# Attention and a gated MLP on one core: the second of four sequences in chunks of 384 tokens in place of 256, with the gating products' second slot and the value means in other places

## The chip, the cores and the metric

The kernel runs on one core of a Trainium2 chip. The metric is the device time of one execution in microseconds (us). The engines are named as the profile names them: PE multiplies matrices (PEld is its loading of weights), DVE, ACT and POOL work element by element, and SP issues DMAs here, one after the other and in the order of its program; a DMA whose buffer or data is not ready holds up every DMA behind it on SP. Each engine has such an order of its own.

## The reference

Two steps. First an attention over 4 sequences, 8 heads, 768 positions and 64 values a head, in which each query sees the keys within 15 positions of it and, for the whole sequence, 24 summaries, one for each block of 32 positions: the maximum of the keys in the block and the mean of the values.

```python
k_sum = k.reshape(B, H, nb, block, D).max(axis=3)
v_sum = v.reshape(B, H, nb, block, D).mean(axis=3)
scores_l = scale * np.matmul(q, k.transpose(0, 1, 3, 2))
mask_l = np.abs(pos[:, None] - pos[None, :]) < window      # window = 16
scores_s = scale * np.einsum('bhsd,bhnd->bhsn', q, k_sum) + np.log(block)
scores_all = np.concatenate([np.where(mask_l, scores_l, -1e9), scores_s], axis=-1)
a = softmax(scores_all)
out = np.matmul(a, np.concatenate([v, v_sum], axis=2))
```

Then a gated MLP over the 3072 rows of 512 that come out: `(x @ w_a) * (x @ w_b) @ w_out`, with 1536 hidden values. All is in fp32.

## The kernel before

**The MLP.** The 3072 tokens are 24 tiles of 128, six for each sequence, and the tiles are grouped in chunks of two (256 tokens, "narrow") or three (384, "wide"). `chunks` lists them: the first two sequences have three narrow chunks each, the last two have two wide ones each, ten in all. For a chunk `u` the MLP runs over 12 blocks `f` of 128 hidden values; one pair (u, f) is an item. All weights stay in SBUF. To reach fp32 precision each operand is split in a high and a low part, and a product is made of three: an item has 24 up products on PE (L1046, `h<-x,w`, 12 for each of w_a and w_b; `late` is the same input at another place), then the gating on ACT and DVE (copy, multiply, and the split of the result into `gh` and `gl`), and later the down products (L1123, `o<-w,gh`, `gl` and `x`), 3 for each of its tiles. In narrow items the gating products have two slots, taken in turn; the second slot, `last`, lies in a ninth place of the input buffer `xt`, so the profile calls it x. Wide items use one slot, of full width. When a chunk's twelfth item is done, its tiles are copied from PSUM to SBUF (L1169, L1175) and stored (`out_dram<-S`, one DMA for each tile).

**The attention of a chunk** is done while the MLP of earlier chunks runs. For each tile: load the queries (`qin<-in_q`), transpose them on DVE (L998, `qT<-qin`), scores on PE (L637, `c<-kT,qT`), softmax on DVE, ACT and POOL, transposes of the weights on DVE (L774, `pt<-s`), values on PE (L790, `o<-pt,vw`), and the split of the result into the chunk's inputs `x`. The buffer qin holds two tiles. A narrow chunk loads its queries for both tiles at once, in 16 DMAs of 32x8x32 elements (32 KB), a wide one tile by tile, in 16 DMAs of 32x4x32 (16 KB). The values of a tile and the summaries stand together in vw, which has one buffer: its three loads for a tile (`vw<-in_v`) follow the value product of the tile before. At the beginning of a sequence its keys are loaded, transposed and reduced (`prep_keys`), and its value means are made (`prep_values`): loads of v into S (`S<-in_v`), sums on POOL into vm, eight small DMAs, one for each head, from vm to a place in S (`S<-vm`, `summed(b)`), and from there two DMAs into vw (`vw<-S`).

**The order.** The kernel is written out by a small planner, `Work`. Every operation has a rank, an assumed duration, and the names of what it reads and writes; the planner gives each engine, when it is free, the ready operation of lowest rank, and so fixes the order of each engine's program. The first operations of each engine follow a list of numbers, `ORDER`, which the change leaves as it is. The planner takes 0.45 us for the issue of any load on SP. Ranks of SP's loads: 90 for S<-in_v and out_dram, 97 for vw, 98 for queries, 99 for S<-vm. An operation "-" takes no engine; it stands for a wait on all that it names.

Of the kernel before, what the change touches and what calls it, by code (L numbers as in the profile page):

```python
# [136 lines left out]
def attention_moe(  # L137
# [11 lines left out]
    B, H, S, D = q.shape  # L149
    P = 128  # L150
# [6 lines left out]
    NS = S // BLK  # L157
# [3 lines left out]
    G = CH // P  # L161
    WIDE = 3

    chunks = [(b, t, n) for b, n in enumerate((G, G, WIDE, WIDE)) for t in range(0, S // P, n)]
    NU = len(chunks)
    CV = 512
    AHEAD = (15, 19, 35)
# [4 lines left out]
    FILL = 2  # L172
# [64 lines left out]
        nc.vector.memset(vbuf[e], 0.0)  # L237
    nc.vector.memset(sbuf[:, :, :, COLS:], 0.0)
    xt = sb([P, 9, NP, P], "x", F32R)
    last = xt[:, 8].rearrange("p c x -> p (c x)")  # L240
    gt, ght, glt = sb([P, 2 * CH], "g"), sb([P, WIDE * P], "gh", F32R), sb([P, WIDE * P], "gl", F32R)
    gs = [gt[:, i * CH : (i + 1) * CH] for i in range(2)]
    ghs, gls = [ght[:, :CH], last[:, :CH]], [glt[:, :CH], last[:, CH:]]
# [20 lines left out]
    def homes_of(u):  # L264
        n = chunks[u][2]
        if u <= FILL:
            return [[f"X{u % 2 * 2 * G + p * G + i}" for i in range(n)] for p in range(2)]
        if u % 2:
            return [[f"X{6 + i}" for i in range(n)], [f"S0.{i}" for i in range(n)]]
        return [[f"X{p * WIDE + i}" for i in range(n)] for p in range(2)]  # L270
# [8 lines left out]
        return late[0][:, : len(names)]  # L279

    def summed(b):
        x = spaces["S0"][:NS, 2 * CV : 3 * CV] if b == 1 else spaces["S1"][4 * NS : 5 * NS, 3 * CV :]
        return x.rearrange("p (h d) -> p h d", d=D)

    def slot(space, i):
        return spaces[space][:, i * 512 : (i + 1) * 512], f"{space}.{i}"
# [32 lines left out]
    def load(rank, kb, rate, reads, writes, out, in_):  # L319
        work.add(  # L320
            "SP", rank, 0.45, kb, reads, writes,
            lambda: nc.sync.dma_start(out=out, in_=in_), rate=rate,  # L322
        )
# [183 lines left out]
    def prep_keys(b):  # L507
        rank = LATER + 2 * b - 0.5
        if b == 1:
            work.add("-", 0, 0, 0, (), ["S1.2", "S1.3", "S0.2", *PU], lambda: None)  # L510
        for c in range(NP):
            i = c % 2 if b == 1 else 0
            kw = kins[i]
            more = (["lo25"], ["S1.2", "S1.3"])[i]
            keys = blocks(96, f"kin{i}", kw, k, b, c, -16, more) + more * i
            groups = kw[:, :S].rearrange("p (i x) -> p i x", x=P)
            for takes, o, i in (
                (0.7, kper[:, c, :, :WIN], groups[:, :, :WIN]),
                (0.26, kper[:, c, :, COLS:], groups[:, :, WIN:]),
                (0.15, kT[:, c, KC - 32 :], kw[:, S:]),  # L520
            ):
                dve(
                    rank, takes, keys, [f"kT{c}k"] + (KB if b == 1 else []),
                    lambda o=o, i=i: nc.vector.transpose(out=o, in_=i),
                )

            hv = half.rearrange("p i x -> p (i x)")
            x16 = "p i (n x) -> p i n x"
            for takes, o, i in (
                (0.65, half[:, :, :6], kper[:, c, :, :WIN].rearrange(x16, x=16)),  # L530
                (0.26, half[:, :, 6:], kper[:, c, :, COLS:].rearrange(x16, x=16)),
                (0.1, ks[:, c, NS - 1, None], kT[:, c, KC - 32 : KC - 16]),
            ):
                dve(
                    rank, takes, [f"kT{c}k"], [f"ks{c}", "half"],
                    lambda o=o, i=i: nc.vector.tensor_reduce(out=o, in_=i, axis=AX.X, op=ALU.max),
                )
            last = ks[:, c, NS - 1, None]
            for takes, o, i0, i1 in (
                (0.26, ks[:, c, : NS - 1], hv[:, 1 : 2 * NS - 2 : 2], hv[:, 2 : 2 * NS : 2]),  # L540
                (0.1, last, last, hv[:, 2 * NS - 1, None]),
            ):
                dve(
                    rank, takes, (), [f"ks{c}", "half"],
                    lambda o=o, i0=i0, i1=i1: nc.vector.tensor_tensor(
                        out=o, in0=i0, in1=i1, op=ALU.max
                    ),
                )
            summaries(rank, c)

    def prep_values(b):


        T = 8

        at, keys, rank = (0, ["S1.0", "S1.1"], LATER) if b == 1 else (3, ["S1.3"], 50)
        x = spaces["S1"][: 4 * NS, at * CV :]

        def add(n, out, i0, i1, writes):
            pool(  # L560
                rank, 0.15 + n / 450, (), writes,
                lambda: nc.gpsimd.tensor_tensor(out=out, in0=i0, in1=i1, op=ALU.add),  # L562
            )

        room = ["S0.2"] if b == 1 else []
        for hg in range(2):
            vv = v[b, 4 * hg : 4 * hg + 4].rearrange("h (n t) d -> (h n) t d", t=BLK)
            y, pk = vm[: 4 * NS, hg], f"vm{hg}"
            for i in range(BLK // T):
                j = i % len(keys)  # L570
                load(
                    90, 197.0, 150, (), [keys[j]],
                    x[:, j * T * D : (j + 1) * T * D].rearrange("p (t d) -> p t d", d=D),
                    vv[:, i * T : (i + 1) * T, :],
                )
                if j == len(keys) - 1:
                    n = len(keys) * T * D // 2
                    while n > D:
                        add(n, x[:, :n], x[:, :n], x[:, n : 2 * n], keys)
                        n //= 2  # L580
                    if i == j:
                        add(n, y, x[:, :n], x[:, n : 2 * n], keys + [pk])
                    else:
                        add(n, x[:, :n], x[:, :n], x[:, n : 2 * n], keys)
                        add(n, y, y, x[:, :n], keys + [pk])
            pool(
                rank, 0.37, (), [pk],
                lambda y=y: nc.gpsimd.tensor_scalar(
                    out=y, in0=y, scalar1=1.0 / BLK, scalar2=None, op0=ALU.mult
                ),  # L590
            )
            for h in range(4):
                load(
                    99, 6.0, 20, [pk] + room, [VS[4 * hg + h]],
                    summed(b)[:, 4 * hg + h], y[h * NS : (h + 1) * NS],
                )
# [182 lines left out]
    def products(u, t, vw, vk, bk, pt=None):  # L779

        rank = rank_of(u)
        ps = bank[bk].rearrange("p (c x) -> p c x", x=P)
        d, dk = pt or PD

        def fn():
            for c in range(NP):
                for e in range(2):
                    es = slice(e * QT, (e + 1) * QT)
                    for h in range(2):
                        nc.tensor.matmul(  # L790
                            ps[h * D : (h + 1) * D, c, es], vw[e][:COLS, 2 * c + h, :],
                            d[:COLS, h, c, es], start=True, stop=True, tile_position=(0, h * D),
                        )

        def split():
            i = t - chunks[u][1]
            hk, lk = (names[i] for names in homes_of(u))
            also = []
            if u == FILL + 1:
                also = PU + [f"S0.{j}" for j in range(4) if j != i] if i == 0 else []  # L800

            y = ps.rearrange("p c (b a) -> p c a b", a=2)

            def home(part):
                return inputs_of(u, part)[:, i].rearrange("p c (a b) -> p c a b", a=2)

            act(
                CHAIN if u > FILL else rank, 0.52, [bk], [hk] + ["gh1", "gl1"] * (hk == "X8"),
                lambda: nc.scalar.copy(out=home(0), in_=y),
            )  # L810
            dve(
                CHAIN if u > FILL else rank, 0.6, [bk, hk], [lk] + (also if i == 0 else []),
                lambda: nc.vector.tensor_tensor(
                    out=home(1), in0=y, in1=home(0).bitcast(F32), op=ALU.subtract
                ),
            )

        return dk[0] + dk[1] + vk, bk, fn, split
# [144 lines left out]
    def attention(u):  # L963
# [18 lines left out]
        def bring(i):  # L982
            load_values(b, t0 + i, vbuf, VK[:3], 97)
            if t0 == 0 and i == 0:
                for e, r0 in ((0, WIN), (1, 32)):
                    load(97, 49.0, 100, VS + (["S0.2"] if b == 1 else []), [VK[3 + e]], vbuf[e][r0 : r0 + NS], summed(b))

        def begin(i):
            keys = list(qk)
# [72 lines left out]
    def item(n, u, f):  # L1062
# [27 lines left out]
        else:  # L1090
# [4 lines left out]
            gk, bk, end = ["g0", "g1"], "h1", n == total - 1  # L1095
            if end:

                bk, ghk, glk = "c1", "X0", "X1"
                pb = bank[bk][:, :W]
                gh, gl = (xt[:, i].rearrange("p c x -> p (c x)")[:, :W] for i in range(2))  # L1100
            for nm, ps, hk in (("a", pa, "h0"), ("b", pb, bk)):
                pe(
                    n - (1.55 if end and nm == "b" else 0), 12 * 0.163, xk + weight_key(f, nm), [hk],
# [136 lines left out]
```

## Time and profile before

| | us |
|---|---|
| median of 3 runs | 665.83 |
| the runs | 665.54, 665.83, 666.66 |
| the profiled execution, its own time | 666.73 |
| its span | 664.6 |
| PE busy | 644.6 (97%) |
| DVE, ACT, POOL busy | 405.8, 247.6, 156.4 |
| DMA moved | 54.76 MB, 82 GB/s over the span |

The profile is of one execution. Its span runs from the first to the last instruction; the execution's own time is 2.1 us longer than it. "Busy" is the time in which an engine had an instruction in work. In the timeline of SP a row is a run of like issues: start, duration from the first to the end of the last, and their number. In an order of instructions, a row is a run of like instructions in an engine's program, with the line, what is written and read, the shape of one, and the count; numbers behind a name tell buffers apart. Line numbers between L280 and L510 are one lower in the changed kernel (L322 is L321 there); from L666 on they are the same.

### The profile page before, as it was taken

What the parts mean: (1) busy time and instruction counts of PE and PEld (TensorE: products, weight loads), DVE (VectorE), ACT (ScalarE), POOL (GpSimd) and SP (SyncE); (2) the same over time, 40 slices, a digit from 0 to 9 for tenths busy, and PEclk for the clock granted to TensorE, in tenths of its full rate; (3) what the DMA queues carried; (4) which work ended last, traced back from release to release, by engine and by line L of the source; (5) the groups of instructions that cost most, each with busy time, mean ns of one, the idle gap of its engine ahead of it and who ended that gap; (6) DMA issues with size and microseconds to landing.
All of it is one profiled execution on the core that took longest, in us unless ns stands there. A gap on an engine that the chain in (4) does not pass through costs nothing.

```text
span 664.6 us, 13879 instructions
## 1 busy us (share of the span) xinstructions
PE 644.6 (97%) x5384; PEld 604.2 (91%) x5384; DVE 405.8 (61%) x905; ACT 247.6 (37%) x748; POOL 156.4 (24%) x236
## 2 busy tenths in 40 slices
PE   5789999999999999999999999999999999999997
PEld 4589898999999999999999999999999999999996
DVE  4787798846777778477667774777762631122212
ACT  3798695323434332234334311343331411121111
POOL 4768476421443333011111100111110100000000
PEclk9789999999999999999999999999999999999999
DMA  9998993254343234423212322132110200010001
GB/s 201 259 305 192 353 261 73 79 112 107 81 81 95 66 78 102 66 44 77 42 37 41 83 42 46 32 81 41 25 25 1 70 1 1 1 47 1 1 1 47
DMA packets 153897, 54.76 MB, mean 82 GB/s; under 512 B 133976, under 2 KB 146520, under 8 KB 153832
## 3 DMA queue, kind: packets, MB, share of 16 engines
q1 hardware_dynamic: 153688, 53.75, 33.9%
q8 instruction: 42, 0.69, 0.4%
q14 instruction: 23, 0.19, 0.1%
q10 hardware_dynamic: 144, 0.13, 0.1%
HBM read 47.12 MB, written 6.29 MB: 80 GB/s over the span
## 4 chain that ended last, share of the span: by engine, by line
PE 83%; SPq 6%; DMA 6%; DVE 3%; issue 1%; ACT 0%; ACTq 0%
PE h L1046 51%; PE o L1123 26%; SPq L322 4%; DMA raw<-in_moe_w_a_dram 3%; PE o L790 3%; PE c L637 3%; SPq L360 2%; DMA raw<-in_moe_w_b_dram 2%; DVE S L396 1%; DVE c L388 1%; DMA raw<-in_moe_w_out_dram 1%; PE c L790 0%; PE c L1046 0%; DVE h L1081 0%; ACT S L385 0%
## 5 line engine op out<-in xcount | busy, mean ns | idle before, releaser
L1046 PE MATMUL h<-x,w 128*128 128x256 f32 (+1 forms) x2488 | 395.9, 295 | 0.0
L1046 PEld LDWEIGHTS h<-x,w 128*128 128x128 f32 x2488 | 355.8, 191 | 4.8 <-issue 0.3
L1046 PE MATMUL h<-late,w 128*128 128x256 f32 (+1 forms) x380 | 114.1, 300 | 0.0
L1123 PE MATMUL o<-w,gh 128*128 128x512 f32 x426 | 106.8, 382 | 0.0
L774 DVE STREAM_TRANSPOSE pt<-s 32x256 f32<-32x256 f32 x228 | 99.3, 436 | 10.8 <-POOL s L729 6.7
L729 POOL TENSOR_TENSOR s<-s,nml 128x480 f32<-128x480 f32 x44 | 43.4, 988 | 224.1 <-DVE nml L725 204.2
L1109 DVE TENSOR_TENSOR h<-h,g 128x384 f32<-128x384 f32 x47 | 26.6, 567 | 109.5 <-PE h L1046 109.3
L1123 PEld LDWEIGHTS o<-w,gh 128*128 128x128 f32 x426 | 76.7, 189 | 9.1 <-issue 1.3
L1111 ACT CAST gh<-h 128x384 fp32r<-128x384 f32 x47 | 22.5, 479 | 151.8 <-DVE h L1109 149.0
L703 ACT ACTIVATE s<-s,nml 128x120 f32<-128x120 f32 x160 | 61.1, 384 | 35.7 <-DVE nml L674 35.1
L1046 PEld LDWEIGHTS h<-late,w 128*128 128x128 f32 x380 | 72.3, 190 | 1.1
L1078 ACT COPY g<-h 128x256 f32<-128x256 f32 x72 | 26.8, 373 | 115.1 <-PE h L1046 115.1
L1123 PE MATMUL o<-w,gl 128*128 128x512 f32 x213 | 59.9, 381 | 0.0
L1081 DVE TENSOR_TENSOR h<-h,g 128x256 f32<-128x256 f32 x72 | 31.1, 432 | 47.0 <-ACT g L1078 46.0
L1123 PE MATMUL o<-w,x 128*128 128x512 f32 x225 | 56.2, 384 | 0.4 <-POOL w L404 0.4
L562 POOL TENSOR_TENSOR S<-S 96x256 f32<-96x256 f32 (+3 forms) x58 | 33.2, 573 | 55.6 <-DMA S<-in_v_dram 52.7
L1123 PEld LDWEIGHTS o<-w,x 128*128 128x128 f32 x225 | 40.0, 189 | 6.4 <-POOL w L404 0.7
L1123 PEld LDWEIGHTS o<-w,gl 128*128 128x128 f32 x213 | 39.9, 189 | 6.1 <-issue 0.3
L1106 ACT COPY g<-h 128x384 f32<-128x384 f32 x48 | 23.0, 479 | 40.0 <-PE h L1046 39.6
L1114 DVE TENSOR_TENSOR gl<-h,gh 128x384 fp32r<-128x384 f32 x47 | 26.2, 556 | 17.5 <-ACT gh L1111 17.1
L666 DVE SCALAR_TENSOR_TENSOR s<-c,mask 128x480 f32<-128x480 f32 x40 | 26.0, 652 | 14.3 <-PE c L637 14.0
L404 POOL TENSOR_TENSOR w<-S,w 128x512 fp32r<-128x512 f32 x24 | 30.8, 1290 | 8.9 <-ACT w L401 8.3
(132 smaller groups left out, 573.5 us busy)
## 6 DMA issues: line engine op xcount, KB each, us to landing
raw<-in_moe_w_b_dram SPq DMA_DIRECT2D x12, 512.0 KB
raw<-in_moe_w_a_dram SPq DMA_DIRECT2D x12, 512.0 KB
raw<-in_moe_w_out_dram SPq DMA_DIRECT2D x12, 512.0 KB
out_dram<-S SPq DMA_DIRECT2D x23, 256.0 KB
S<-in_v_dram SPq DMA_DIRECT2D x24, 192.0 KB
kin<-in_k_dram SPq DMA_DIRECT2D x38, 100.0 KB
vw<-in_v_dram SPq DMA_DIRECT2D x17, 192.0 KB
qin<-in_q_dram SPq DMA_DIRECT2D x192, 16.0 KB
```

What stands on the lines that cost most here:

```text
L322: lambda: nc.sync.dma_start(out=out, in_=in_), rate=rate,
L404: lambda eng=nc.vector if near else nc.gpsimd: eng.tensor_tensor(out=half(1), in0=t, in1=half(0).bitcast(F32), op=ALU.subtract),
L562: lambda: nc.gpsimd.tensor_tensor(out=out, in0=i0, in1=i1, op=ALU.add),
L703: lambda h=h, c=c, more=more: nc.scalar.activation(y[h][:, c, :], x[h][:, c, :], AF.Exp, bias=m[:, 0, h, c : c + 1], scale=1.0, **more,),
L729: lambda h=h, r=r: nc.gpsimd.tensor_tensor(out=y[h], in0=y[h], in1=r[:, :, None].broadcast_to([P, NP, COLS]), op=ALU.mult,),
L774: lambda js=js, qs=qs, rs=rs: nc.vector.transpose(out=pv[js, rs, qs], in_=sv[qs, rs, js]),
L1046: nc.tensor.matmul(ps, w[:, c, part, :], inputs_of(u, xpart)[:, :, c].rearrange("p g (a b) -> p g b a", a=2), start=(i == 0), stop=(i == n ...
L1078: act(CHAIN, 0.38, [hk], [gk], lambda: nc.scalar.copy(out=g, in_=pa))
L1081: lambda: nc.vector.tensor_tensor(out=pa, in0=pb, in1=g, op=ALU.mult),
L1109: lambda: nc.vector.tensor_tensor(out=pb, in0=pb, in1=g, op=ALU.mult),
L1114: lambda: nc.vector.tensor_tensor(out=gl, in0=pb, in1=gh.bitcast(F32), op=ALU.subtract),
L1123: nc.tensor.matmul(bank[ok[j]], (gh if first else gl)[:, j * P : (j + 1) * P], w[:, :, part, :].rearrange("p (z a) n -> p z n a", a=2), st ...
```

## The change

The second sequence's tiles are grouped as 3 + 3 in place of 2 + 2 + 2, so there are 9 chunks and 108 items (36 narrow, 72 wide) in place of 10 and 120. With that go moves of buffers: the second slot of the gating products lies in place 0 of `xt` in place of 8, and the inputs of the first three chunks begin at place 1; the last item's gating products lie in places 6 and 7; and the value means of every later sequence lie in one piece of S (`S1`, rows 96 to 119 of its last quarter), where those of the third and fourth lay already, in place of a piece of `S0` for the second sequence. The "-" operations that hold back loads into those places name the new places: the second sequence's key loads no longer wait for `S0.2` and `PU` (the transposed weights of the third chunk's second tile).

```diff
-    chunks = [(b, t, n) for b, n in enumerate((G, G, WIDE, WIDE)) for t in range(0, S // P, n)]
+    chunks = [(b, t, n) for b, n in enumerate((G, WIDE, WIDE, WIDE)) for t in range(0, S // P, n)]
...
-    last = xt[:, 8].rearrange("p c x -> p (c x)")
+    last = xt[:, 0].rearrange("p c x -> p (c x)")
...
         if u <= FILL:
-            return [[f"X{u % 2 * 2 * G + p * G + i}" for i in range(n)] for p in range(2)]
+            return [[f"X{1 + u % 2 * 2 * G + p * G + i}" for i in range(n)] for p in range(2)]
...
     def summed(b):
-        x = spaces["S0"][:NS, 2 * CV : 3 * CV] if b == 1 else spaces["S1"][4 * NS : 5 * NS, 3 * CV :]
-        return x.rearrange("p (h d) -> p h d", d=D)
+        return spaces["S1"][4 * NS : 5 * NS, 3 * CV :].rearrange("p (h d) -> p h d", d=D)
...
         if b == 1:
-            work.add("-", 0, 0, 0, (), ["S1.2", "S1.3", "S0.2", *PU], lambda: None)
+            work.add("-", 0, 0, 0, (), ["S1.2", "S1.3"], lambda: None)
...
-        room = ["S0.2"] if b == 1 else []
+        room = ["S1.3"] if b == 1 else []
+        work.add("-", 0, 0, 0, (), room, lambda: None)
...
-                CHAIN if u > FILL else rank, 0.52, [bk], [hk] + ["gh1", "gl1"] * (hk == "X8"),
+                CHAIN if u > FILL else rank, 0.52, [bk], [hk] + ["gh1", "gl1"] * (hk == "X0" and u > FILL),
...
-                    load(97, 49.0, 100, VS + (["S0.2"] if b == 1 else []), [VK[3 + e]], vbuf[e][r0 : r0 + NS], summed(b))
+                    load(97, 49.0, 100, VS + (["S1.3"] if b == 1 else []), [VK[3 + e]], vbuf[e][r0 : r0 + NS], summed(b))
...
-                bk, ghk, glk = "c1", "X0", "X1"
+                bk, ghk, glk = "c1", "X6", "X7"
...
-                gh, gl = (xt[:, i].rearrange("p c x -> p (c x)")[:, :W] for i in range(2))
+                gh, gl = (xt[:, i].rearrange("p c x -> p (c x)")[:, :W] for i in (6, 7))
```

## The prediction

> **What bounds the kernel now.** I read the page's busy shares first, then the waits of TensorE (PE), then windows around the second sequence's attention, and last the chain of waits for the length of one item.
>
> ```profile
> PE 644.6 (97%) x5384; PEld 604.2 (91%) x5384; DVE 405.8 (61%) x905; ACT 247.6 (37%) x748; POOL 156.4 (24%) x236
> ```
>
> ```profile
> PE o L421 <- DMA space<-in_k_dram: 4.2, 1, 4.2
> PE c L637 <- DVE qT L998: 1.3, 1, 1.3
> ```
>
> ```profile
> 160.00:180.00 20.00, 20.00 (x218) 18.29 (x216) 15.39 (x36) 8.50 (x34) 6.56 (x13) 1.00 0.31 69
> 180.00:200.00 20.00, 20.00 (x201) 18.89 (x200) 15.06 (x36) 8.62 (x35) 9.33 (x16) 1.00 0.41 84
> 400.00:660.00 260.00, 260.00 (x1798) 246.21 (x1796) 108.97 (x232) 66.85 (x195) 12.48 (x14) 1.00 0.10 24
> ```
>
> PE is busy 97% of the span; its waits (us in total, times, longest) lie in the first stage, and in the windows (PE busy is the second number) every microsecond is a PE microsecond at a granted clock of 1.00. So from 140 us on two things alone change the time: fewer PE microseconds, or a wait on PE. A wait is not made up later, since nothing behind it has slack.
>
> **What the wide chunks save.** The chain of waits gives one item of each width (start, us; 24 up products, then the down products):
>
> ```profile
> 146.19 2.68 PE h L1046 x24
> 148.86 1.30 PE o L1123 x6
> 150.16 2.68 PE h L1046 x24
> ...
> 586.06 3.90 PE h L1046 x24
> 589.96 1.94 PE o L1123 x9
> 591.90 3.90 PE h L1046 x24
> ```
>
> A narrow item (256 tokens) lasts 150.16 - 146.19 = 3.97 us, a wide one (384 tokens) 591.90 - 586.06 = 5.84 us. The second sequence had 3 chunks x 12 blocks = 36 narrow items, 36 x 3.97 = 142.9 us, and gets 2 x 12 = 24 wide ones, 24 x 5.84 = 140.2 us: **-2.76 us**. Scores and values go by tiles of 128 tokens and stay six. ACT and DVE do fewer, longer gating operations in cover: beside PE's 260.00 us the last window has 108.97 us of DVE and 66.85 of ACT. The new slot of the gating products, and the last item's, change an address and no instruction; the move of the means costs nothing of itself either (8 small DMAs from vm, 2 to vw, as before). What these edits move is the order on SP, the engine that issues the DMAs.
>
> **What the change moves on SP.** The second sequence's value means go from vm to S and from there to vw, and the first value product (L790, `o<-pt,vw`) reads them. Before, around them on SP:
>
> ```order
> L322 DMA S_147<-vm 24x64 x7
> L322 DMA S_146<-in_k_dram 32x25x32 x4
> L322 DMA S_147<-vm 24x64
> L322 DMA kin<-in_k_dram 32x25x32 x2
> L322 DMA out_dram<-S_147 128x512 x2
> L322 DMA kin<-in_k_dram 32x25x32 x2
> L322 DMA vw_129<-S_147 24x512
> L322 DMA vw_130<-S_147 24x512
> L322 DMA S_146<-in_v_dram 96x512 x2
> L322 DMA qin<-in_q_dram 32x8x32 x12
> ```
>
> With the change:
>
> ```order
> L321 DMA out_dram<-S_147 128x512 x2
> L321 DMA vw_129<-in_v_dram 80x8x64
> L321 DMA vw_130<-in_v_dram 32x8x64
> L321 DMA vw_130<-in_v_dram 64x8x64
> L321 DMA S_146<-vm 24x64 x3
> L321 DMA S_146<-in_v_dram 96x512 x2
> L321 DMA S_146<-vm 24x64
> L321 DMA qin<-in_q_dram 32x4x32 x30
> L321 DMA out_dram<-S_147 128x512 x2
> L321 DMA qin<-in_q_dram 32x4x32 x34
> L321 DMA S_146<-vm 24x64 x4
> L321 DMA vw_129<-S_146 24x512
> ```
>
> A wide chunk loads its queries tile by tile, 16 DMAs of 16 KB each, where a narrow one takes 16 of 32 KB for two tiles: 96 issues for the sequence instead of 48. 32 of them come earlier, and 64 now stand ahead of the last four vm copies and of vw<-S; there were none there.
>
> On PE the values of the first tile before (o_71/72: down products; the second fence is with the change):
>
> ```order
> L1046 MATMUL h_75<-x,w_1064 128x256 x12
> L1046 MATMUL h_75<-x,w_1020 128x256 x12
> L1123 MATMUL o_71<-w_1011,x 128x512 x2
> L1123 MATMUL o_72<-w_1011,x 128x512 x2
> L790 MATMUL o_74<-pt,vw_129 64x64 x2
> ```
>
> ```order
> L1123 MATMUL o_71<-w_870,gl 128x512
> L1123 MATMUL o_72<-w_870,gl 128x512
> L1046 MATMUL h_75<-x,w_1064 128x256 x12
> L1046 MATMUL h_75<-x,w_1020 128x256 x12
> L790 MATMUL o_74<-pt,vw_129 64x64 x2
> ```
>
> They stay right behind the same pair of up products (w_1064 and w_1020), and lose the half down product that stood between: PE is not asked to come later.
>
> **When PE arrives.** Both orders are alike up to the 48 up products that end here:
>
> ```profile
> 135.56 5.36 PE h L1046 x48
> 140.91 1.30 PE o L1123 x6
> ```
>
> ```profile
> 160.72 1.05 PE L637 MATMUL c<-kT,qT 64*64 64x120 f32 x32
> 161.70 1.13 PE L1123 MATMUL o<-w,gh 128*128 128x512 f32 x4
> ```
>
> From there to L790 the new order has three scores (161.70 - 160.72 = 0.98 each; one more than before, the third tile now belongs to this chunk), 8 pairs of up products at 2.68 and 8 down at 1.30: 140.91 + 2.94 + 21.44 + 10.40 = **175.7**. Before it came at 175.86.
>
> **When the means arrive.** SP's own timeline (start, us, number of issues), first those around the means, then runs of the 16 KB query loads:
>
> ```profile
> 105.14 0.81 SPq L322 DMA_DIRECT2D qin<-in_q_dram  x2
> ...
> 134.07 1.39 SPq L322 DMA_DIRECT2D out_dram<-S  x2
> ...
> 136.04 1.02 SPq L322 DMA_DIRECT2D S<-in_v_dram  x2
> ...
> 138.78 3.26 SPq L322 DMA_DIRECT2D vw<-in_v_dram  x3
> ...
> 155.47 1.51 SPq L322 DMA_DIRECT2D vw<-S  x2
> ...
> 165.28 5.76 SPq L322 DMA_DIRECT2D qin<-in_q_dram  x12
> ...
> 196.13 1.77 SPq L322 DMA_DIRECT2D vw<-in_v_dram  x3
> ```
>
> ```profile
> 284.86 1.65 SPq L322 DMA_DIRECT2D vw<-S  x2
> 287.88 3.00 SPq L322 DMA_DIRECT2D S<-vm  x4
> 290.98 8.56 SPq L322 DMA_DIRECT2D qin<-in_q_dram  x16
> 299.64 3.04 SPq L322 DMA_DIRECT2D S<-vm  x4
> 304.64 8.20 SPq L322 DMA_DIRECT2D qin<-in_q_dram  x15
> 312.94 0.85 SPq L322 DMA_DIRECT2D out_dram<-S  x2
> ...
> 323.10 7.74 SPq L322 DMA_DIRECT2D qin<-in_q_dram  x16
> ...
> 341.26 8.26 SPq L322 DMA_DIRECT2D qin<-in_q_dram  x16
> ...
> 383.02 8.48 SPq L322 DMA_DIRECT2D qin<-in_q_dram  x16
> ```
>
> ```profile
> L322 SPq DMA_DIRECT2D qin<-in_q_dram x96: 312/430/1472, 291.0 to 391.1; - x96
> ```
>
> Before, the means were issued by 156.98, 18.9 us ahead of their use; that slack hid everything here. Now: the five query runs take 41.24 us for 79 issues, **0.522 us each** (the last row, min/median/max in ns: most take 430 ns, some a microsecond more, and every run of 15 or 16 has its share). A run that started at 287.88 had to wait until vw<-S, issued by 284.86 + 1.65 = 286.51, had landed: 1.37 us for the landing of such a small move.
>
> The start: out_dram waits for the copies of the first chunk's results, made behind PE work whose order is the same, so it stays at 134.07, if SP is there by then. From 105.14, where queries start to flow in the trace of before, the new order puts 32 queries (16.7 us), 6 S<-in_v, 12 key loads and 3 vw (11 us at about 0.5) ahead of it: 132.9. Just in time; each microsecond more would add to the sum.
>
> 134.07 + out 1.39 + vw x3 1.77 + vm x4 3.04 + in_v x2 1.02 = 141.3; + 64 x 0.522 = 33.4 makes 174.7; + out 0.85 + vm x4 3.04 = 178.6; + landing 1.37, + vw<-S 1.65, + landing 1.37 = **183.0**. The queries' buffer, which holds two tiles, is no further brake: the last 16 queries (sixth tile) need the fourth tile's transpose, which follows the third tile's scores, on PE until about 161; SP gets there at 141.3 + 48 x 0.522 = 166.4.
>
> PE waits from 175.7 to 183.0, **+7.3 us**. Queued behind L790 on PE is every later product, so all of it is lost. An earlier wait (at the scores, if keys or queries come late) would eat into these 7.3, not add.
>
> Bounds of that wait. The fastest pitch in the rows is 0.48 (165.28: 5.76 / 12; 323.10: 7.74 / 16): 30.7 us in place of 33.4. The other landing that SP waited for is in its waits (total, times, longest):
>
> ```profile
> SPq L322 <- DMA vw<-S: 1.3, 2, 0.8
> ```
>
> With two landings of 0.8 in place of 1.37 the wait is 3.5. Upwards, the slowest pitch (0.535, at 290.98) adds 0.8, a vw load like that at 138.78 adds 1.5, and SP late by 1 us at the start adds 1: 10.6. I take 7.3, from the mean over 79.
>
> The Trainium skill, "DMA: Bandwidth & Descriptors", section on the anatomy of one DMA, gives a fixed cost of about 2.0 us for each DMA, most of it the receipt of the write, fitted on DMAs from GpSimd. By it the two landings in series would be 4.0 in place of 2.74, the wait 8.6 and the time 671.6; the row of 1.37 speaks for less.
>
> **Sum.** -2.76 + 7.28 = +4.5 us. The profiled execution took 666.73 us (span 664.6), so with the change 671.2; the median of the runs, 665.83, lies 0.9 below it: **670.3 us**.
>
> **Rivals.** (A) *The means are in time: faster.* One mechanism: SP issues the 64 queries fast enough that vw<-S lands by 175.7. All else in the sum is 149.6, which leaves 26.1 / 64 = 0.408 us a query. No wait, and the gain stands: 663.1. For it: single pairs near that pitch can be had, the fastest issue was 312 ns. Against it: no run of 12 or more is under 0.48, and the four vm copies and two landings follow serially. 0.12.
> (B) *Wait and gain cancel.* At 28.9 / 64 = 0.451 us a query the wait is 2.8 and the time 665.8. Closer than A to the rows, still under the floor of 0.48, unless landings or vm copies are cheaper too: 0.13.
> (C) *A second wait.* Values of tiles two and three reload vw, whose three DMAs can be issued only once the L790 before has read it, and S<-in_v loads that wait for POOL's sums stand between them on SP. One such pair held SP 4.40 us:
>
> ```profile
> 157.08 4.40 SPq L322 DMA_DIRECT2D S<-in_v_dram  x2
> ```
>
> Between the first and second L790 PE has two pairs of up and two down products, 5.36 + 2.60 = 8.0 us; 1.1 for L790, 1.77, 4.40 and a landing of 1.37 make 8.6, 0.7 over; and after a late start POOL and SP have work heaped up, so I put it at 1 to 3 us more, 671.3 to 673.3. 0.13.
> (D) *The change does not do what it says*: a wide item saves nothing here and the wait stands alone, 673.1. Both durations come from one run at one clock, so 0.02.
>
> **How the numbers follow.** Forecast 0.60, A 0.12, B 0.13, C 0.13, D 0.02. A measurement here tells about 0.2%, 1.3 us, from no change: faster (under 664.5) is A, 0.12; no change is B, 0.13; slower (over 667.2) is the rest, 0.75. The likeliest case's own range is 666.5 (wait 3.5) to 673.7 (wait 10.6); the range stretches down into B, to 664.8, and ends at 673.6; A and the rare mishap beyond stay out.
>
> **What would show it.** In the profile after: a row in which PE's L790 waits for the DMA vw<-S (or for what issued it) of about 7 us near 176 to 183; one long train of 16 KB queries on SP from about 141 to 175 with vw<-S at about 180; wide items of 5.84 us for the second sequence; no other PE wait over 1 us after 110. If vw<-S is issued before 172, or that train runs under 0.45 us a query, I am wrong towards A; if the longest wait is at L637, or L790 waits for pt, I have the wrong late thing; if L790 waits twice, it is C.

## The result, and the profile after

The changed kernel takes 673.04 us (median of 6 executions, 672.0 to 675.08) against 666.32 for the kernel before beside it: a ratio of 1.0104, 95% interval 1.0088 to 1.0120. It is slower by 6.7 us; the forecast was 4.5, its range 664.8 to 673.6. The profiled execution took 675.08 us (span 673.3) and is the longest of the six; against the profiled one of before that is 8.35 us more, and the tables below add up to that.

PE's waits in the changed kernel (us in total, times, longest), those of the first stage left out:

```profile
PE o L790 <- DMA vw<-S: 5.6, 2, 5.4
...
PE c L637 <- DVE qT L998: 1.5, 1, 1.5
PE c L637 <- DVE s L666: 1.3, 2, 0.8
```

The first line is the wait that was forecast; the second lies at 106 us and has its like before (1.3). SP's timeline in the changed kernel, from the first chunk's results to the means:

```profile
135.63 1.47 SPq L321 DMA_DIRECT2D out_dram<-S  x2
137.19 1.67 SPq L321 DMA_DIRECT2D vw<-in_v_dram  x3
138.96 2.50 SPq L321 DMA_DIRECT2D S<-vm  x3
141.55 0.92 SPq L321 DMA_DIRECT2D S<-in_v_dram  x2
142.52 0.75 SPq L321 DMA_DIRECT2D S<-vm  x1
143.38 15.74 SPq L321 DMA_DIRECT2D qin<-in_q_dram  x30
159.22 0.85 SPq L321 DMA_DIRECT2D out_dram<-S  x2
160.12 18.36 SPq L321 DMA_DIRECT2D qin<-in_q_dram  x34
178.58 3.05 SPq L321 DMA_DIRECT2D S<-vm  x4
182.90 1.48 SPq L321 DMA_DIRECT2D vw<-S  x2
```

The train of 64 queries takes 15.74 + 18.36 = 34.1 us, 0.533 a query, and vw<-S stands behind it; before it was issued at 155.47. On PE the same stretch reads:

```profile
160.61 1.58 PE L1123 MATMUL o<-w,x 128*128 128x512 f32 x6
162.66 0.42 PE L637 MATMUL c<-kT,qT 64*64 64x120 f32 x4 [0.46 <-DVE s L666]
163.91 1.04 PE L637 MATMUL c<-kT,qT 64*64 64x120 f32 x28 [0.83 <-DVE s L666]
164.88 1.13 PE L1123 MATMUL o<-w,gh 128*128 128x512 f32 x4
...
176.91 2.84 PE L1046 MATMUL h<-x,w 128*128 128x256 f32 x24
185.11 0.48 PE L790 MATMUL o<-pt,vw 120*64 120x64 f32 x4 [5.37 <-DMA vw<-S]
185.78 1.76 PE L790 MATMUL o<-pt,vw 120*64 120x64 f32 x28 [0.19 <-DMA vw<-S]
187.47 2.76 PE L1123 MATMUL o<-w,x 128*128 128x512 f32 x6
190.07 1.03 PE L1123 MATMUL o<-w,gh 128*128 128x512 f32 x4
```

The up product at 176.91 takes 2.68, so PE was free for L790 at 179.59. L790 (1.08 when nothing holds it) and six down products (1.30) were done at 190.07 in place of 181.97: 8.1 us lost, of which the wait is 5.56. The other 2.5 us are PE's own: L790 and the six products behind it took about double. The windows say why (PE busy is the second number, the granted clock the last but two):

```profile
180.00:184.00 4.00, 0.00 (x0) 0.00 (x0) 0.43 (x1) 0.58 (x2) 0.00 (x0) 0.89 0.04 6
184.00:188.00 4.00, 2.70 (x33) 2.40 (x34) 0.55 (x2) 0.41 (x1) 0.95 (x2) 0.50 0.25 74
188.00:192.00 4.00, 4.00 (x18) 3.39 (x17) 3.85 (x9) 0.18 (x1) 1.00 (x3) 0.76 0.59 148
192.00:196.00 4.00, 4.00 (x38) 4.00 (x38) 2.62 (x7) 0.74 (x2) 1.36 (x4) 1.00 0.16 49
```

During the wait the clock fell to half, and it stayed there for the first microseconds of work behind it.

The chain of waits has, ahead of this stretch:

```profile
137.11 5.37 PE h L1046 x48
```

The whole difference, in this execution: PE came to the 48 up products of the third chunk 1.55 late, at 137.11 against 135.56 in the chains of waits; at L637 of the third tile, due at 160.61 + 1.30 = 161.91 and done at 164.88, 2.0 were lost; at L790 8.1. That is 11.65; less the gain of the wide chunks, 2.76, it makes 8.9, and 8.35 was measured (8.7 in the span); the 0.5 between them stay open.

### The profile page after: what moved, and what is told of

The parts are those of the page before. It is cut to its first block, busy times and chain, and to the rows that moved or that the text cites. A ratio compares the mean times of both kernels' runs of the same rounds, so it can differ in the third digit from the quotient of the medians.

```text
span 673.3 us, 13320 instructions
## 1 busy us (share of the span) xinstructions
PE 646.2 (96%) x5096; PEld 603.3 (90%) x5096; DVE 401.9 (60%) x880; ACT 244.5 (36%) x725; POOL 156.4 (23%) x236
## 3 DMA queue, kind: packets, MB, share of 16 engines
q1 hardware_dynamic: 154456, 53.75, 33.4%
## 4 chain that ended last, share of the span: by engine, by line
PE 77%; SPq 7%; DMA 6%; DVE 5%; issue 2%; ACT 1%; POOL 1%; POOLq 0%; ACTq 0%; DVEq 0%
PE h L1046 46%; PE o L1123 24%; SPq L321 7%; PE o L790 3%; DMA raw<-in_moe_w_a_dram 3%; PE c L637 2%; DMA raw<-in_moe_w_out_dram 2%; DVE S L774 1%; POOL w L403 1%; DVE pt L774 1%; DVE c L387 1%; DVE S L395 1%; DVE h L1081 1%; PE o L624 0%; PE o L637 0%
## 5 line engine op out<-in xcount | busy, mean ns | idle before, releaser
L1046 PE MATMUL h<-x,w 128*128 128x384 f32 (+1 forms) x2292 | 392.0, 307 | 0.0
L1123 PE MATMUL o<-w,gh 128*128 128x512 f32 x498 | 123.8, 383 | 0.1
L1109 DVE TENSOR_TENSOR h<-h,g 128x384 f32<-128x384 f32 x71 | 40.2, 566 | 134.8 <-PE h L1046 134.4
L1123 PEld LDWEIGHTS o<-w,gh 128*128 128x128 f32 x498 | 90.6, 189 | 11.5 <-issue 1.9
L1046 PE MATMUL h<-late,w 128*128 128x384 f32 x288 | 93.9, 326 | 0.0
L1046 PEld LDWEIGHTS h<-late,w 128*128 128x128 f32 x288 | 54.4, 189 | 0.9
L1123 PE MATMUL o<-w,x 128*128 128x512 f32 x117 | 30.9, 400 | 0.6 <-POOL w L403 0.5
L703 ACT ACTIVATION_READ_ACCUMULATOR s<-s,nml 128x1 f32 x160 | 30.3, 189 | 0.0
L1078 ACT COPY g<-h 128x256 f32<-128x256 f32 x36 | 13.4, 373 | 46.1 <-PE h L1046 46.1
L387 DVE TENSOR_SCALAR c<-raw 128x512 int32<-128x512 uint32 x36 | 27.3, 761 | 1.6 <-DMA raw<-in_moe_w_a_dram 1.0
```

The lines of the kernel that those rows point to most:

```text
L387: dve(rank, 0.66, [raw], [bk], lambda: nc.vector.tensor_scalar(out=z.bitcast(I32), in0=word(0).bitcast(U32), scalar1=2.0**-29, scalar2=7.0 ...
L703: lambda h=h, c=c, more=more: nc.scalar.activation(y[h][:, c, :], x[h][:, c, :], AF.Exp, bias=m[:, 0, h, c : c + 1], scale=1.0, **more,),
L1046: nc.tensor.matmul(ps, w[:, c, part, :], inputs_of(u, xpart)[:, :, c].rearrange("p g (a b) -> p g b a", a=2), start=(i == 0), stop=(i == n ...
L1109: lambda: nc.vector.tensor_tensor(out=pb, in0=pb, in1=g, op=ALU.mult),
L1123: nc.tensor.matmul(bank[ok[j]], (gh if first else gl)[:, j * P : (j + 1) * P], w[:, :, part, :].rearrange("p (z a) n -> p z n a", a=2), st ...
```

## Experiments

The theory (Q) is that the means are late because of the number of DMA issues ahead of them on SP. The rivals: the means are late by themselves, through POOL or their new place (M); the wide chunks save nothing (W); and, for the last pair of runs, that other edits make the gain (E).

**Take 16 issues out of the train, or put 16 in.** Both leave the order of everything else as it is. The loads in question are those of the second sequence's sixth tile.

```diff
-    def load(rank, kb, rate, reads, writes, out, in_):
+    def load(rank, kb, rate, reads, writes, out, in_, times=1):
...
-            lambda: nc.sync.dma_start(out=out, in_=in_), rate=rate,
+            lambda: [nc.sync.dma_start(out=out, in_=in_) for _ in range(times)], rate=rate,
...
                             ap=[[D, rows], [32 * D, m], [1, 32]],
                         ),
+                        0 if rank == 98 and (b, row) == (1, 5 * P) else 1,
```

This is d16, in `blocks`, which issues the queries; p16 has 2 in place of 0. Lines from L450 on are one higher in these two kernels than in the changed one.

> The changed kernel without the loads of the second sequence's sixth tile of queries (they are left out, so that tile's scores are computed from the fourth tile's queries); every other instruction keeps its place. Theory Q (the value means are late because they stand on SP behind 64 query loads): the train has 48 loads, 16 x 0.53 = 8.5 us less, vw<-S lands near 177.3, before PE comes to L790 (179.6 in the changed kernel's trace); no wait there, granted clock 1.00 from 180 to 200, time about 665 us (673.0 - 8.1). Rival M (the means are late by themselves: POOL's sums or their new place in S): the wait stays at about 5 us, time 672 to 673.

Measured: 665.86 us, ratio 0.9996 (0.9986 to 1.0006). L790 doesn't wait and the clock stays at 1.00, since the means are issued ten microseconds earlier, as SP's timeline of this kernel has it:

```profile
158.50 9.38 SPq L321 DMA_DIRECT2D qin<-in_q_dram  x18
167.98 3.05 SPq L321 DMA_DIRECT2D S<-vm  x4
172.30 1.48 SPq L321 DMA_DIRECT2D vw<-S  x2
```

M falls: POOL's sums, the place of the means and the width of the chunks are unchanged, and the wait is gone. The 7.2 us by which this kernel is faster than the changed one are about the wait and the slow clock behind it (8.1 in the profiled execution). It doesn't get below the kernel before, because the 2 us at L637 stay (its waits still have `PE c L638 <- DVE s L667: 1.3, 2, 0.8`).

> The changed kernel with the same 16 query loads issued twice; every other instruction keeps its place. Theory Q: vw<-S moves from 182.9 to about 191.4, the wait at L790 grows from 5.6 to 14 us, time 681 to 683 us: 8.5 more, and no more than 1 us beside it if the slow clock behind the wait costs the same for a longer wait. Rival M: time within 1 us of 673.

Measured: 699.5 us, ratio 1.0503 (1.0482 to 1.0524): 26.5 more than the changed kernel, not 8.5. The direction is Q's, the dose was not what I took it for. The waits of PE, and those of SP, in this kernel:

```profile
PE o L791 <- DMA vw<-S: 31.8, 2, 31.6
```

```profile
SPq L321 <- DMA qin<-in_q_dram: 21.8, 16, 2.6
```

A second load into the same place waits on SP until the first has landed, 16 times, 21.8 us in all; with the issues themselves the train grew by 44.74 - 18.36 = 26.4 us (the 50 issues begin at 158.04). The wait at L790 grew by 31.8 - 5.6 = 26.2 and the time by 26.5. So what delays vw<-S on SP arrives in the kernel's time one for one, and the slow clock cost about the same behind 32 us as behind 5.6.

**Put the means ahead of the queries.** First by their rank; then also with SP's true prices in the planner.

```diff
-                    99, 6.0, 20, [pk] + room, [VS[4 * hg + h]],
+                    96 if b == 1 else 99, 6.0, 20, [pk] + room, [VS[4 * hg + h]],
```

> The changed kernel with one rank changed: the second sequence's S<-vm loads get rank 96 (before queries, 98) in place of 99. Planned anew, 19 query loads stand ahead of the last four S<-vm and of vw<-S in place of 64, and L790 of the first tile comes earlier on PE, near 160. Theory Q: the means land near 162, the wait is 0 to 2 us, time 663 to 666 us. Rival M: a wait of 5 us or more at L790, time 670 or more. Rival W (a wide chunk does not save its 2.8 us here): 666 to 668 even without a wait.

Measured: 679.18 us, ratio 1.0199 (1.0182 to 1.0216), slower than the changed kernel. No wait for vw<-S is left, as Q expected, but the time fits none of the three expectations: other waits are there. PE's waits in this kernel:

```profile
PE o L1123 <- ACT x L1083: 3.5, 3, 3.1
PE o L1123 <- ACT gh L1083: 3.2, 2, 2.9
...
PE o L790 <- DVE pt L774: 1.7, 1, 1.7
```

L1083 makes the gating products, and it waits for DVE. DVE's timeline before the first of them:

```profile
165.16 0.69 DVE L813 TENSOR_TENSOR late<-o,x 128x512 fp32r<-128x512 f32 x1 [1.48 <-DMA out_dram<-S]
...
169.54 0.71 DVE L998 STREAM_TRANSPOSE qT<-qin 128x512 f32<-128x512 f32 x1 [3.08 <-DMA qin<-in_q_dram]
...
172.70 1.78 DVE L774 STREAM_TRANSPOSE pt<-s 32x256 f32<-32x256 f32 x4 [1.16 <-POOL s L729]
174.51 0.43 DVE L1081 TENSOR_TENSOR h<-h,g 128x256 f32<-128x256 f32 x1
```

The planner used the earlier means to move the values to 160, and what now comes late on SP is a store (the split of the values writes into the place it reads) and the next tile's queries. DVE waits for them in its own order, with the gating of a running item (L1081, at 174.51) behind. The queue on SP is as long as before; only what stands last in it has changed.

```diff
-            "SP", rank, 0.45, kb, reads, writes,
+            "SP", rank, {98: 0.52, 96: 0.76, 99: 0.76}.get(rank, 0.45), kb, reads, writes,
```

> As means_first, and the planner takes 0.52 us for the issue of a query load and 0.76 for S<-vm, as measured, in place of 0.45. 13 query loads stand ahead of the last four S<-vm. Theory Q: the means land near 159, as PE comes to L790; no wait over 0.5 us there, time 662.5 to 664.5 us, faster than the kernel before (666.3). Rival M: as above, 670. Rival W: 666 or more.

Measured: 669.19 us, ratio 1.0046 (1.0030 to 1.0063): better than the change by 3.9 us, slower than before. Its longest wait on PE after the first stage:

```profile
PE c L637 <- DVE qT L998: 5.0, 2, 3.8
```

The means are in time and the queries are not. Neither M nor W, as I had written them, expects a wait there; it is Q's queue again, from its other end: with 96 query issues SP brought both in time in neither of these two orders.

**Halve the issues.** Wide chunks, those of the third and fourth sequence too, load their queries for two tiles at once, as narrow ones do: the same bytes, 48 issues for a sequence. The order is planned anew.

```diff
             if n != G:
-                for c in range(NP):
-                    keys += blocks(
-                        98, f"q{(t0 + i) % 2}.{c}", qin[:, c, place(i)], q, b, c, (t0 + i) * P, (),
-                        old if chunks[u - 1][2] == G and i < 2 else (),
-                    )
+                keys += old
+                if (t0 + i) % 2 == 0:
+                    for c in range(NP):
+                        blocks(98, f"qin.{c}", qin[:, c, :], q, b, c, (t0 + i) * P)
```

> The changed kernel, but wide chunks load their queries for two tiles at once, in 16 DMAs of 32 KB as narrow ones do: 48 query issues for the second sequence in place of 96, the same bytes, planned anew. 16 query loads stand ahead of the last S<-vm and vw<-S. Theory Q (lateness comes from the number of issues on SP): the means land near 157, PE comes to the first L790 near 160; no wait over 0.5 us there, the gain of the wide chunks appears: 662 to 664.5 us. Rival W (wide chunks do not save 2.8 us here): 665.5 or more. Rival D (the wait moves to the queries' transposes, since pairs load later): 664.5 to 667 with waits at L637.

Measured: 666.22 us, ratio 1.0007 (0.9995 to 1.0019), 6.8 under the changed kernel. PE comes to L790 19 us earlier here than in the changed kernel, and still waits a little for the means:

```profile
162.31 0.34 PE L790 MATMUL o<-pt,vw 120*64 120x64 f32 x4 [1.54 <-DMA vw<-S]
162.99 1.04 PE L790 MATMUL o<-pt,vw 120*64 120x64 f32 x28 [0.34 <-DMA vw<-S]
163.96 1.05 PE L637 MATMUL c<-kT,qT 64*64 64x120 f32 x32
```

The 28 products take 1.04 here and took 1.76 in the changed kernel: after a wait of 1.9 us the clock is still full. My expectation of no wait was off by those 1.9 us, which use up most of the gain. An issue of 32 KB takes SP hardly longer than one of 16 KB (a run of 16 has 8.88 us in this trace, 0.555 each), so on SP the number of issues counts here, and hardly their bytes.

> As pairs, and with both edits of means_first_real_costs: the second sequence's S<-vm rank ahead of queries, the planner takes 0.52 us for a query issue and 0.76 for S<-vm. 3 query loads stand ahead of the last four S<-vm. Theory Q: no PE wait over 0.5 us after 120, time 662 to 664 us, faster than before by 0.3 to 0.6%. Rival W: 665.5 or more.

Measured: 663.95 us, ratio 0.9967 (0.9957 to 0.9977): faster than the kernel before. Of PE's waits after 120 us one of 0.2 is left, and the first values find their means there:

```profile
152.84 1.48 SPq L321 DMA_DIRECT2D vw<-S  x2
```

```profile
157.00 1.15 PE L790 MATMUL o<-pt,vw 120*64 120x64 f32 x32
```

The same kernel measured again, beside the control that follows:

> The kernel of pairs_means_first_real_costs once more, beside narrow_same_edits: 663 to 665 us, 0.2 to 0.5% under the kernel before.

Measured: 663.48 us, ratio 0.9959 (0.9943 to 0.9975).

> The kernel before, chunks 2, 2, 3, 3 and places as they were, with the three edits that pairs_means_first_real_costs has beside the change (queries in pairs, means' rank, the planner's costs of SP). Theory Q: before had no PE wait after 120 us to take away, so it stays at 665.5 to 667; the 2.2 us by which pairs_means_first_real_costs is faster are those of the wide chunks. Rival E (the three edits make the gain, the wide chunks nothing): 663 to 664.5 us.

Measured: 666.27 us, ratio 1.0002 (0.9992 to 1.0013). The three edits alone do nothing for the narrow chunks, so E falls: what pairs_means_first_real_costs gains, 2.2 and 2.3 us in the two comparisons, 2.8 against this control, comes with the change. The control has the old places as well as the old chunks, so it doesn't tell one from the other; but the new places alone save nothing (next runs), and the wide items are as short as forecast (their rows stand further down). So W falls too.

**Each part of the change alone.** With the new places under the old chunks, and with the old places under the new ones, some inputs and gating products share a place at a time, so part of the values computed in these two kernels is another; their instructions are as many and of the same kinds.

```diff
-    chunks = [(b, t, n) for b, n in enumerate((G, WIDE, WIDE, WIDE)) for t in range(0, S // P, n)]
+    chunks = [(b, t, n) for b, n in enumerate((G, G, WIDE, WIDE)) for t in range(0, S // P, n)]
```

> The kernel before with every line of the change but the first: chunks stay 2, 2, 3, 3; slot and means move. Theory Q: 16 query loads of 32 KB ahead of vw<-S, no long wait, no gain either: 665 to 667.5 us, within 0.2% of before or little over. Rival M (the means' new place makes them late): a wait of 4 us or more at L790 and 670 us or more.

Measured: 670.46 us, ratio 1.0073 (1.0053 to 1.0092). More than Q expected; the time is at M's bound (670), but the wait at the first L790 is 1.6 us in place of M's 4 or more:

```profile
162.55 1.30 PE L790 MATMUL o<-pt,vw 120*64 120x64 f32 x32 [1.61 <-DMA vw<-S]
```

The move of the places does cost, but through the order: the keys may load earlier, so PE comes to the first values of the sequence at about 161 in place of 175.9, and the 18.9 us by which the means were early are gone. This wait, and one of 0.8 at a later L790 for pt, explain 2.4 of the 4.3 us. PE is 0.5 late by the 48 up products (136.03 against 135.56); where the rest lies stays open.

```diff
-    chunks = [(b, t, n) for b, n in enumerate((G, G, WIDE, WIDE)) for t in range(0, S // P, n)]
+    chunks = [(b, t, n) for b, n in enumerate((G, WIDE, WIDE, WIDE)) for t in range(0, S // P, n)]
```

> The kernel before with only the first line of the change: the second sequence in wide chunks, slot and means where they were. The order on SP has vw<-S behind 4 late query loads, but the second sequence's key loads behind the third chunk's values (as before), and on PE all three score steps of the chunk between 160 and 190 with the value steps right behind each other. Theory Q: no wait for vw<-S, but waits at L637 for keys or queries and at L790 for the softmax, 5 us or more in all: 670 us or more. Rival M: without the moved means the time is 663 to 666 us.

Measured: 703.54 us, ratio 1.0564 (1.0548 to 1.0580), as expected in kind. PE's waits in this kernel:

```profile
PE o L790 <- DVE pt L774: 24.3, 6, 6.3
PE c L637 <- POOL kT L456: 4.5, 1, 4.5
```

With the means in the old place the keys come late, and all the sequence's attention is pressed into some 40 us with hardly an item to cover it, and the granted clock is 0.50 from 176 to 208. So the two parts need each other, and the new places are not the fault by themselves: with them and 48 issues the time is that of before, with 96 it is 6.8 us more.

## Why the prediction was right, and where it was off

**The gain of the wide chunks, -2.76: right.** 663.95 and 663.48 against 666.27 for the control with the same edits is -2.3 and -2.8. The second sequence's wide items last 262.50 - 256.66 = 5.84 us in the changed kernel's chain of waits, as forecast:

```profile
256.66 3.90 PE h L1046 x24
260.56 1.94 PE o L1123 x9
262.50 3.90 PE h L1046 x24
```

Rival D falls.

**The price of a query issue, 0.522: right.** The train's 64 took 34.1 us for the 33.4 of the sum, and min/median/max in it are 312/430/1659 ns, so the long ones came too. Rivals A (0.408) and B (0.451) needed a pitch that no train in these traces has.

**The start, 134.07: right, though 1.6 late in the profiled execution.** There out_dram went out at 135.63. In d16 and p16, whose order up to the train is the same, it went out on time:

```profile
134.27 1.20 SPq L321 DMA_DIRECT2D out_dram<-S  x2
```

```profile
133.94 1.49 SPq L321 DMA_DIRECT2D out_dram<-S  x2
```

PE's lateness divides likewise. At the scores at 106 us it is 0.96 (106.13 against 105.17 before), but d16 and p16 have 104.77 and 104.45 there: that is scatter of the first stage. From there to the 48 up products PE takes 30.98 us in the changed kernel, 30.98 and 30.97 in d16 and p16, and 30.39 before, so 0.6 us belong to the new order. Of these, 0.36 lie at a value product (133.82 to 135.27; before 132.85 to 133.94) that in the chain of waits stands right behind DVE's transposes. DVE is busier in the new order, 38.44 of the 40 us from 100 to 140 against 31.89 before. That the keys, freed of their wait, are the reason is argued and not shown.

**Two landings of 1.37 each: right.** S<-vm ended at 178.58 + 3.05 = 181.63 and vw<-S was issued at 182.90; that one ended at 184.38 and L790's second part ran from 185.78: 1.27 and 1.40. The Trainium skill's figure of about 2.0 us a DMA ("DMA: Bandwidth & Descriptors", anatomy of one DMA) fits the same rows if it is counted from the beginning of the issue: the chain of waits has 1.83 and 2.07 us from there. Added behind the issue, as my sentence in the prediction did, it counts the issue twice.

**An earlier wait eats into the 7.3: right in kind.** The 2.0 us at L637 are one. DVE, in its order, waited for the third tile's queries, the first 16 of the train, and the transposes and maxima behind that came late:

```profile
153.45 0.71 DVE L998 STREAM_TRANSPOSE qT<-qin 128x512 f32<-128x512 f32 x1 [2.74 <-DMA qin<-in_q_dram]
```

PE arrived at L790 3.9 us later than forecast (1.6 + 2.0 + 0.3), the means 2.8 later, and so PE stood idle there for 5.6, not 7.3. What is lost before the wait is lost all the same: 9.1 us for start and waits together.

**"All of it is lost": too little.** This is the step that failed. The term for the wait left out the work behind it, which runs at half clock: 2.5 us. In the profiled execution 8.35 stand against the forecast 4.5; of the 3.8 between them the late start is 1.4 to 1.7 (135.63 against d16 and p16), and the rest is about the size of the slow clock. The median exceeds the forecast by 2.2, but of its six executions only this one has a trace. The prediction looked at the rows from 140 us on, where PE had no wait. The first stage of before has one of 3.5 us at L742 and, in the same stretch, a granted clock of 0.75:

```profile
PE o L742 <- POOL s L729: 3.8, 2, 3.5
```

```profile
20.00:40.00 20.00, 14.87 (x176) 12.03 (x176) 16.23 (x34) 16.27 (x43) 15.64 (x22) 0.75 1.06 272
```

A page could have shown it too: the Trainium skill, "TensorE: Matmul & The Clock Gate", Part 1, says that PE's clock goes to half after an idle window of some 3.4 us and comes back after a busy one of that length. By that rule an estimate of the term is 1.7 us at least (half of 3.4). The traces agree: 0.50 in the window from 184 to 188 above, and full speed again 5 us after the first product.

**Rival C, a second wait, did not come:** the next two value products started without one.

## What to carry to other kernels

A change that splits loads into smaller ones must be priced in issues of the queue that issues them, at the pitch which long runs in the trace show (0.52 us here, not the 0.43 of the median issue or the 0.45 of the planner), and what stands last in that queue is then compared with its use. Moving one thing forward in a full queue makes another late (means_first); fewer issues for the same bytes took most of it away (pairs), and with both and true prices in the planner the gain came out (pairs_means_first_real_costs). And a stall of the bound engine should be priced with the slow start behind it.

## What the runs showed of the hardware

PE's clock behind a wait: after 1.6 us (places_only) and 1.9 us (pairs, in two parts) it stayed at 1.00. After 3.1 us, in means_first, six down products took 2.7 us in place of 1.30:

```profile
175.40 2.93 PE L1123 MATMUL o<-w,x 128*128 128x512 f32 x6 [3.10 <-ACT x L1083]
178.12 3.16 PE L1046 MATMUL h<-x,w 128*128 128x256 f32 x24
```

In all 1.8 us were lost behind this wait, 1.8 behind 3.8 us (means_first_real_costs), 2.5 behind 5.6 (the change), and 3.1 behind 31.8 (p16). So one long wait costs some 2 to 3 us more, and the price hardly grows with its length. Read as a mix of 1.00 and 0.50, the windows give an estimate of how long the half clock lasted: 0.89, 0.50 and 0.76 from 180 to 192 in the changed kernel make 0.9 + 4.0 + 1.9 = 6.8 us, and 0.92 and 0.65 from 172 to 180 in means_first make 3.4. The loss is about half of the time that PE worked in such a stretch.

How short a wait is enough, these runs do not fix. means_first has a second one, of 2.9 us:

```profile
211.79 1.13 PE L1123 MATMUL o<-w,gh 128*128 128x512 f32 x4 [2.93 <-ACT gh L1083]
```

These four products ran at full speed, and the clock is at 0.50 in the window from 213 to 214. In the first stage of the kernel before, where PE's waits lie close together, it is 0.89 from 36 to 37 and 0.50 from 37 to 40, right after a wait of 1.8 us. The window of 3.4 us in the Trainium skill ("TensorE: Matmul & The Clock Gate", Part 1) agrees with the slow stretches of 3.4 and 6.8 us, while the clock fell here after waits shorter than it.

A DMA that writes where one before it in the same queue writes waited at SP for that one's landing in p16: 1.4 us each (21.8 / 16), on top of the issue.
